# Moving LSH bit rows from SBUF straight into the operand tile, one transfer per bit, for pairs 1 to 5

## The chip, the cores and the metric

The kernel runs on one core of one Trainium2 chip. The metric is device time in microseconds (us), lower is better. Executions of one kernel spread by about one per cent here, so a ratio below 1.01 means little by itself; intervals are given at 95%. One execution of each kernel was taken by the profiler; "the profile" and "the trace" are of that one.

## The reference

Two stages. Attention over 4 batches, 8 heads, 768 tokens, 64 elements a head: a query sees only the keys that share its 6-bit hash.

```python
q_bits = (np.einsum('bhsd,dk->bhsk', q, proj) > 0)          # same for k_bits
mask = q_bucket[:, :, :, None] == k_bucket[:, :, None, :]   # all 6 bits agree
scores = np.where(mask, scale * np.matmul(q, k.transpose(0, 1, 3, 2)), -1e9)
attn = softmax(scores); out = np.matmul(attn, v)
```

Its output, as 3072 tokens of 512, goes through a feed-forward part: `h = max(max(x @ w1, x @ w2), x @ w3)`, then `h @ w_out`, with 768 hidden units.

## The kernel before

The mask costs no work on the scores: the 6 bits, coded as plus or minus a large number, stand as 6 extra rows below the 64 rows of q and k in the operand tile `T`, so that the score matmul adds a large constant for each bit that agrees, and the exponential takes away all but full agreement. Heads are worked on in pairs (16 of them, 4 to a batch; "pair 4" is the first of the second batch). Per pair: load q and k (fp32), split each into two fp16 parts (VectorE and ScalarE), transpose on TensorE into `T`, multiply by the projection (`hps`), compare with zero on VectorE (`bit`), transpose the bits (`bps`), shift and scale them (`bt`), and bring these rows into partitions 64 to 69 of `T`. The rows have to come from 72 partitions into 6 others, and two transfers do it, through DRAM:

```python
    def hash_bits(b, pr, e):
        ...
        nc.vector.tensor_tensor(out=bit[:].rearrange("p n a k -> p (n a) k"), in0=hv[:, :, 0:NBITS], in1=neg[:],
                                op=AluOp.is_gt)          # 128 x (q/k, chunk, bit): the bit runs fastest

    def bit_T(b, pr, e):                                 # TensorE: two transposes of 128 x 72
        ...
    def bit_evac(b, pr, e):                              # VectorE: bt, 72 x 2 x 128
        ...
    def bit_out(b, pr, e):
        drs[b, pr] = dram.tile([2, R, P], FP16, tag="dr", name="dr")
        nc.sync.dma_start(drs[b, pr][:].rearrange("n r t -> r n t"), bts.pop((b, pr))[:])

    def bit_in(b, pr, e):
        nc.sync.dma_start(T[b, pr][D : D + NBITS, :, :],
                          drs.pop((b, pr))[:].rearrange("n (a k) t -> k (n a) t", k=NBITS))
```

The kernel carries its own list scheduler: each piece is a task with an engine, an assumed duration, a priority and its buffers, and a simulated clock decides the order in which each engine's instructions are written down. On the chip that order is fixed, and each engine executes what is written for it in that order. The tasks concerned:

```python
        bo = add(("SP", 0.65), p0 + 7, [be], lambda e: bit_out(b, pr, e), take=("dr",), give=("bt",), xfer=0.05,
                 after=[last_copy[0]])
        bi = add(("SP", 0.65), p0 + 7, [bo], lambda e: bit_in(b, pr, e), give=("dr",), xfer=0.25, ...)
        # loads of q, k, v of later batches are issued on the same queue, behind the bits of an earlier pair:
        loads[n, b, pr, (0, 2)] = add(("SP", 0.5), ..., after=[last_load[0], bounced[g], ...])
```

The softmax here doesn't subtract the row's maximum and nothing guards it: scores larger than these inputs give would overflow.

## Time and profile before

| | before |
|---|---|
| time, median of 3 | 268.71 us (267.62 to 270.26) |
| span of the profiled run | 265.3 us |
| TensorE busy | 97% |
| pair 1's bits ready, its first scores | 18.9 us, 26.38 us |
| next batch's first loads issued (q, k; the following v) | 26.96, 27.41; 32.84 us |
| first layer-1 matmul of the feed-forward part | 48.74 us |
| one comparison (`bit`) on VectorE | 0.31 us |

In the lines below, L and a number is a line of that kernel, SPq the queue of SyncE that issues transfers (it works in order, and its times are issue times, not transfer times); `out<-in` names the tiles; a bracket is idle time of that engine just before, with what ended it. Tiles named often: `s` the fp16 parts of q and k ("splits"), `tps` transposes, `sc` scores, `AT` their exponentials, `av` attend, `svp` and `vsum` the sum of v that is added with a small weight ("mean"), `ps` and `po` layers 1 and 2 of the feed-forward part. A "unit" is one pair of score matmuls with its exponential. The prediction shows the lines of before on which it rests.

### The profile page before, as it was taken

The page shows a single profiled execution, that of the slowest core. Times are in us where ns is not written, and L with a number is a line of the kernel's source. Part 1 is how long each engine was busy: PE and PEld are TensorE (multiplying, and loading weights), DVE is VectorE, ACT ScalarE, POOL GpSimd, SP SyncE. Part 2 cuts the span into 40 slices and gives each one's busy share as a digit, 9 for nine tenths or more (in the row PEclk, how much of TensorE's full clock was granted, in tenths as well). Part 3 has the DMA queues.
Part 4 walks back from the last instruction along what each step waited for, and adds up shares of the span by engine and source line. Part 5 has one row for each costly group of instructions (what it writes and reads, how often), then busy time and mean ns, then how long its engine had stood idle before and what let it go on. Part 6 is the DMA issues. An engine that isn't in the chain of part 4 may idle for free.

```text
span 265.3 us, 7323 instructions
## 1 busy us (share of the span) xinstructions
PE 257.1 (97%) x2992; PEld 174.8 (66%) x2992; DVE 174.4 (66%) x394; ACT 196.2 (74%) x283; POOL 43.0 (16%) x57
## 2 busy tenths in 40 slices
PE   7997999999999999999999999999999999999995
PEld 7886777767656666676666767766666656565552
DVE  5999489999747897468984795551655526255260
ACT  5897799997926889989989899888898632332322
POOL 1421063273310334003321030000000000000000
PEclk9999799999999999999999999999999999999999
DMA  7994489799998798989896885302030060120303
GB/s 225 340 271 80 132 278 261 236 210 325 228 216 264 209 245 199 231 226 202 172 228 186 233 173 106 70 14 97 24 62 0 4 178 4 40 79 0 121 0 120
DMA packets 67409, 41.69 MB, mean 157 GB/s; under 512 B 48047, under 2 KB 63663, under 8 KB 67375
## 3 DMA queue, kind: packets, MB, share of 16 engines
q1 hardware_dynamic: 64654, 39.26, 57.3%
q0 software_dynamic: 2640, 1.97, 4.8%
q8 instruction: 23, 0.38, 0.6%
q14 instruction: 12, 0.09, 0.1%
q10 hardware_dynamic: 80, 0.00, 0.0%
HBM read 25.72 MB, written 6.84 MB: 123 GB/s over the span
## 4 chain that ended last, share of the span: by engine, by line
PE 80%; DMA 8%; ACT 4%; POOL 2%; SPq 2%; DVE 1%; issue 1%; ACTq 0%; POOLq 0%
PE ps L478 31%; PE sc L395 21%; PE po L496 11%; PE av L413 11%; DMA v<-in_v_dram 5%; ACT AT L401 3%; PE hps L312 3%; DMA ws<-in_moe_w_out_dram 2%; SPq L250 2%; PE tps L292 1%; DMA T<-dr 1%; POOL vt L363 1%; ACT T L202 1%; PE bps L339 1%; DVE xn L449 0%
## 5 line engine op out<-in xcount | busy, mean ns | idle before, releaser
L401 ACT ACTIVATE AT<-sc 128x768 f16<-128x768 f32 x192 | 146.3, 815 | 15.9 <-PE sc L395 14.0
L478 PE MATMUL ps<-xT,w_sb 128*128 128x384 f16 x576 | 106.3, 326 | 0.1
L395 PE MATMUL sc<-T 128*128 128x384 f16 x384 | 94.0, 328 | 2.4 <-DMA T<-dr 1.4
L487 DVE TENSOR_TENSOR ht<-ht,ps 128x384 f16<-128x384 f16 x96 | 52.9, 551 | 46.6 <-PE ps L478 44.2
L413 PEld LDWEIGHTS <-AT 128*128 128x128 f16 x1152 | 60.1, 98 | 23.1 <-issue 0.7
L478 PEld LDWEIGHTS <-w_sb 128*128 128x128 f16 x576 | 52.7, 98 | 30.3 <-issue 0.2
L413 PE MATMUL av<-vone,AT 128*128 128x65 f16 x1152 | 66.0, 194 | 0.0
L395 PEld LDWEIGHTS <-T 128*128 128x128 f16 x384 | 30.3, 98 | 12.9 <-DMA T<-dr 1.6
L496 PE MATMUL po<-wout_sb,ht 128*128 128x512 f16 (+1 forms) x150 | 33.8, 370 | 0.5 <-POOL wout_sb L204 0.5
L202 ACT CAST ht<-ps 128x384 f16<-128x384 f32 x28 | 13.4, 479 | 26.4 <-DVE ht L487 19.1
L202 ACT COPY osb<-po 128x512 f32<-128x512 f32 (+1 forms) x24 | 13.6, 567 | 18.7 <-PE po L496 18.6
L363 POOL TENSOR_TENSOR vt<-v 128x384 f32<-128x384 f32 x12 | 13.8, 1149 | 65.3 <-DMA v<-in_v_dram 59.2
L430 DVE TENSOR_TENSOR t<-av,mv 128x390 f32<-128x390 f32 x32 | 18.0, 561 | 9.0 <-PE av L413 8.8
L496 PEld LDWEIGHTS <-ht 128*128 128x128 f16 x150 | 14.1, 98 | 14.3 <-DVE rr L436 0.8
L449 DVE TENSOR_TENSOR xn<-t,rr 128x384 f16<-128x384 f32 x32 | 20.0, 625 | 1.1
L273 DVE SCALAR_TENSOR_TENSOR s<-q,s 128x384 f16<-128x384 f32 x32 | 19.0, 609 | 2.5 <-ACT s L266 2.3
L273 DVE SCALAR_TENSOR_TENSOR s<-k,s 128x384 f16<-128x384 f32 x32 | 19.1, 615 | 0.2
L204 DVE CAST ht<-ps 128x384 f16<-128x384 f32 x20 | 11.1, 554 | 10.0 <-PE ps L478 9.7
L292 PE MATMUL tps<-iden,s 128*128 128x128 f16 x168 | 13.3, 219 | 0.9 <-DVE bit L322 0.3
L292 PEld LDWEIGHTS <-s 128*128 128x128 f16 x168 | 10.4, 98 | 2.2 <-DVE s L273 1.1
L312 PEld LDWEIGHTS <-T 128*128 128x128 f16 x336 | 10.0, 96 | 1.0
L312 PE MATMUL hps<-PAB,T 128*128 128x12 f16 x336 | 10.4, 168 | 0.0
(54 smaller groups left out, 141.5 us busy)
## 6 DMA issues: line engine op xcount, KB each, us to landing
v<-in_v_dram SPq DMA_DIRECT2D x16, 384.0 KB
out_dram<-osb SPq DMA_DIRECT2D x23, 256.0 KB
q<-in_q_dram SPq DMA_DIRECT2D x15, 384.0 KB
k<-in_k_dram SPq DMA_DIRECT2D x15, 384.0 KB
w_sb<-in_moe_w_dram POOLq DMA_DIRECT2D x5, 384.0 KB, 10.4
ws<-in_moe_w_out_dram SPq DMA_DIRECT2D x3, 512.0 KB
ws<-in_moe_w_dram SPq DMA_DIRECT2D x2, 384.0 KB
dr<-bt SPq DMA_DIRECT2D x15, 36.0 KB
```

Of the source, the lines that this page charges most:

```text
L202: nc.scalar.copy(o, i)
L273: nc.vector.scalar_tensor_tensor(out=s[:, a0:a1, D : 2 * D], in0=raw_view(n, b, pr, heads), scalar=QS, in1=s[:, a0:a1, 0:D], op0=AluOp.mul ...
L292: nc.tensor.transpose(p16[:, c * P : (c + 1) * P], S16[b, pr][:, a0 + c, :], iden[:])
L312: nc.tensor.matmul(o, T[b, pr][:, a, :], PAB[:], start=True, stop=True)
L395: nc.tensor.matmul(sc[:, i, 0:HQ], t[:, NA2 + hh * NCH + 2 * j + i, :], t[:, hh * NCH + hf * CH : hh * NCH + (hf + 1) * CH, :], start=True ...
L401: nc.scalar.activation(AT[:], scs.pop(u)[:, :, 0:HQ], ActFn.Exp, bias=EXP_BIAS, scale=EXP_SCALE)
L413: nc.tensor.matmul(av[:, o : o + D + 1], AT[:, i, c * P : (c + 1) * P], vones[b % 2][:, 2 * pr + hh, 2 * j + i, 0 : D + 1], start=slot == ...
L430: nc.vector.tensor_tensor(out=t[:, :, :, 0 : D + 1], in0=av[:, :, :, 0 : D + 1], in1=mv, op=AluOp.add)
L449: nc.vector.tensor_tensor(out=xv, in0=t[:, :, :, 0:D], in1=rr[:].to_broadcast([P, 2, CH, D]), op=AluOp.mult)
L478: nc.tensor.matmul(ps[:, 0:HQ], w_sb[i][:, jc, fb * P : (fb + 1) * P], xTs[b, hf][:, jc, :], start=jc == 0, stop=jc == NJ - 1)
L487: nc.vector.tensor_tensor(out=ht[:], in0=ht[:], in1=ps[:, 0:HQ], op=AluOp.max)
L496: nc.tensor.matmul(ps[:, m0:m1], hts[b, hf, fb][:, c * P : (c + 1) * P], wout_sb[:, fb, m0:m1], start=fb == 0, stop=fb == NF - 1)
```

## The change

Its intent: pair 1's scores wait for two transfers in a row. With the bits laid out bit-major, one bit's 24 rows of 128 lie in 24 partitions of `bt` in the order in which one partition of `T` wants them, so that one transfer from SBUF to SBUF places a whole row, without DRAM between. Six transfers replace two, for pairs 1 to 5; the others keep the way through DRAM.

```diff
+    direct = (1, 2, 3, 4, 5)
+
+    def by_chunk(b, pr, bit):
+        if 4 * b + pr not in direct:
+            return bit[:]
+        return bit[:].rearrange("p n a k -> p (n a k)").rearrange("p (k n a) -> p n a k", k=NBITS, n=2)
...
-        nc.vector.tensor_tensor(out=bit[:].rearrange("p n a k -> p (n a) k"), in0=hv[:, :, 0:NBITS], in1=neg[:],
-                                op=AluOp.is_gt)
+        nc.vector.tensor_tensor(out=by_chunk(b, pr, bit), in0=hv[:, :, 0:NBITS].rearrange("p (n a) k -> p n a k", n=2),
+                                in1=neg[:].rearrange("p (n a) k -> p n a k", n=2), op=AluOp.is_gt)
...
+    def bit_move(b, pr, e):
+        bt = bts.pop((b, pr))
+        for i in range(NBITS):
+            h, r = divmod(i, NBITS // 2)
+            nc.sync.dma_start(T[b, pr][D + i : D + i + 1, :, :], bt[r * NA : (r + 1) * NA, h, :])
...
+        if 4 * b + pr in direct:
+            bi = add(("SP", 1.9), p0 + 7, [be], lambda e: bit_move(b, pr, e), give=("bt",), xfer=0.3,
+                     after=[last_copy[0]])
+        else:
             bo = add(("SP", 0.65), ...)          # as before
             bi = add(("SP", 0.65), ...)
```

The scheduler is told 1.9 us for six issues, and with that the order of all engines is planned anew.

More of the change, by code (lines that the diff above doesn't have):

```diff
@@ L319, in hash_bits0 @@
             bits[0, pr] = bit
-            nc.vector.tensor_scalar(out=bit[:], in0=hv, scalar1=0.0, scalar2=None, op0=AluOp.is_gt)
+            nc.vector.tensor_scalar(out=by_chunk(0, pr, bit), in0=hv, scalar1=0.0, scalar2=None, op0=AluOp.is_gt)
             return
@@ L338, in bit_T @@
         for n in range(2):
-            nc.tensor.transpose(p16[0:R, n * P : (n + 1) * P], bit[:, n, :, :].rearrange("p a k -> p (a k)"), iden[:])
+            nc.tensor.transpose(p16[0:R, n * P : (n + 1) * P], bit[:, n, :, :].rearrange("p x y -> p (x y)"), iden[:])
     def bit_evac(b, pr, e):
@@ L627, in prep @@
         be = add(("DVE", 0.28), p0 + 6, [bT], lambda e: bit_evac(b, pr, e), take=("bt",), give=("mm",))
-        bo = add(("SP", 0.65), p0 + 7, [be], lambda e: bit_out(b, pr, e), take=("dr",), give=("bt",), xfer=0.05,
-                 after=[last_copy[0]])
-        bi = add(("SP", 0.65), p0 + 7, [bo], lambda e: bit_in(b, pr, e), give=("dr",), xfer=0.25, pad=3 if 4 * b + pr > 5 else 0.0)
+        if 4 * b + pr in direct:
+            bi = add(("SP", 1.9), p0 + 7, [be], lambda e: bit_move(b, pr, e), give=("bt",), xfer=0.3,
+                     after=[last_copy[0]])
+        else:
+            bo = add(("SP", 0.65), p0 + 7, [be], lambda e: bit_out(b, pr, e), take=("dr",), give=("bt",), xfer=0.05,
+                     after=[last_copy[0]])
+            bi = add(("SP", 0.65), p0 + 7, [bo], lambda e: bit_in(b, pr, e), give=("dr",), xfer=0.25, pad=3 if 4 * b + pr > 5 else 0.0)
         bounced[b, pr] = last_copy[0] = bi
```

## The prediction

> **What bounds the kernel now.** I read the page first (busy shares, the forty slices, the chain that ended last), then the timelines of TensorE, ScalarE and the DMA-issuing queue from 8 to 80 us, then one-microsecond windows around the one hole they show.
>
> Busy shares, slices and the head of the chain, from the page:
> ```profile
> PE 257.1 (97%) x2992; PEld 174.8 (66%) x2992; DVE 174.4 (66%) x394; ACT 196.2 (74%) x283; POOL 43.0 (16%) x57
> PE   7997999999999999999999999999999999999995
> ACT  5897799997926889989989899888898632332322
> PEclk9999799999999999999999999999999999999999
> PE 80%; DMA 8%; ACT 4%; POOL 2%; SPq 2%; DVE 1%; issue 1%; ACTq 0%; POOLq 0%
> ```
> TensorE looks full everywhere, but its slices overlap pipelined matmuls, so 97% is not a proof. In the chain, a pair of score matmuls steps by 0.33 us, six attend matmuls by 0.18, six transposes by 0.34, four layer-1 matmuls by 0.65. From about 48.7 us (first layer-1 matmuls) to the drain the timeline is these steps nearly back to back: the feed-forward part fills every gap that attention leaves. **So after 48.7 us TensorE is the bound, and only less work for it or an earlier start of that phase can shorten the run.** Before it there is attention alone, and ScalarE's exponentials (about 0.75 us each when contiguous) set the pace. The slices that stand out are PEclk's fifth (7; 26.5 to 33 us, as a slice is 6.6 us) and ScalarE's fourth and fifth (7). ScalarE's timeline, with start and duration ahead of each group and idle time behind:
> ```profile
> 24.25 0.80 ACT L202 COPY T<-tps 128x768 f16<-128x768 f16 x1
> 26.97 1.51 ACT L401 ACTIVATE AT<-sc 128x768 f16<-128x768 f32 x2 [1.93 <-PE sc L395]
> 28.78 0.81 ACT L401 ACTIVATE AT<-sc 128x768 f16<-128x768 f32 x1 [0.30 <-PE sc L395]
> 30.08 0.81 ACT L401 ACTIVATE AT<-sc 128x768 f16<-128x768 f32 x1 [0.48 <-PE sc L395]
> 31.26 3.70 ACT L401 ACTIVATE AT<-sc 128x768 f16<-128x768 f32 x5 [0.38 <-PE sc L395]
> ```
> ScalarE loses 1.93 + 0.30 + 0.48 + 0.38 = 3.09 us to scores that came late. TensorE's timeline says why, and the queue's timeline has the two transfers behind it:
> ```profile
> 26.38 0.82 PE L395 MATMUL sc<-T 128*128 128x384 f16 x4 [1.45 <-DMA T<-dr]
> ```
> ```profile
> 18.92 0.38 SPq L349 DMA_DIRECT2D dr<-bt  x1
> 23.99 0.28 SPq L352 DMA_DIRECT2D T<-dr  x1
> 24.35 0.30 SPq L349 DMA_DIRECT2D dr<-bt  x1
> 26.65 0.26 SPq L352 DMA_DIRECT2D T<-dr  x1
> 26.96 0.40 SPq L250 DMA_DIRECT2D q<-in_q_dram  x1
> 30.88 0.32 SPq L349 DMA_DIRECT2D dr<-bt  x1
> 32.50 0.29 SPq L352 DMA_DIRECT2D T<-dr  x1
> ```
> This is pair 1's round trip through DRAM: out at 18.92, the queue held until 23.99 for it to land, back in by 26.38, when the scores go. It holds the queue too: pair 2's bits are ready at 23.66 (start 23.38 + 0.28 of its bt) and go out only at 24.35, and a later load only at 26.96. The windows add a second cost, the columns being busy time and count per engine, granted clock, DMA share and GB/s:
> ```profile
> 23.00:24.00 1.00, 0.85 (x18) 0.77 (x15) 1.00 (x3) 1.00 (x2) 0.00 (x0) 1.00 0.10 15
> 25.00:26.00 1.00, 0.00 (x0) 0.00 (x0) 0.93 (x4) 0.04 (x1) 0.00 (x0) 1.00 0.30 67
> 28.00:29.00 1.00, 1.00 (x12) 0.75 (x10) 0.63 (x3) 0.70 (x2) 0.00 (x0) 0.56 0.91 266
> 29.00:30.00 1.00, 1.00 (x13) 0.66 (x11) 0.36 (x1) 0.59 (x1) 0.00 (x0) 0.50 1.05 366
> ```
> TensorE stands still for one whole window, and soon afterwards its clock is halved for about 3.4 us.
>
> **What the Trainium skill says.** (1) DMA: Bandwidth & Descriptors, section on the anatomy of one DMA: about 2 us of fixed cost, mostly the receipt of the last write, heaviest where the target is HBM (given for the GpSimd path). The trace agrees in size: in a quiet stretch the way out takes 32.50 - 30.88 = 1.62 us and the way in 26.38 - 23.99 = 2.39. (2) Same page, section on why a DMA increments its semaphore by 16: the slowest dimension not of size one decides how many engines work, the largest number up to 16 that divides it on both sides. The transfer back has 6 rows, so 6 engines; a new one-bit transfer has 24 rows of 128 on both sides, so 12. No view of before shows the second. (3) TensorE: Matmul & The Clock Gate, part 1: half the clock after an idle window of some 3.4 us. Here idleness of 1.45 us in a thin stretch was enough for windows of 0.50.
>
> **The change, part by part.**
> - *Bit-major layout.* The same DVE instructions (15 comparisons, 15 evacuations) with another write order; the comparisons take 0.30 to 0.31 us now. Estimate: at most 0.1 us more for each of five, off the path. The matrix transposes stay two per pair.
> - *Removed, for pairs 1 to 5:* one way out, one wait of the queue for it, one way in. For pair 1 the second way is 2.39 us on the path. For the others it is 1.6 to 2.9 us of latency, mostly with slack: pair 4 leaves at 41.91 and returns with an issue at 47.25, yet it is needed only at unit 48.
> - *Added:* six issues a pair. An issue of this queue takes 0.26 to 0.38, with its gap about 0.36, so 6 x 0.36 = 2.2 us instead of 0.38 + 0.28 = 0.66 us of issue. Pair 1's six go from 18.92 to about 21.1. They queue on the same engines behind the loads, as the way out does now, so I have the last one land when the way out lands now, at about 24.0 (window 23 to 24: the engines are nearly empty). **That is 26.38 - 24.0 = 2.4 us earlier.**
> - *Moved:* the order listing shows the scheduler moved work too. The unit that waits (number 13, from one) now stands behind 12 transposes that before ended at about 24.05, and the mean and attend matmuls that filled 24.05 to 24.76 come after it. TensorE should hardly stand still. Between units 13 and 36 ScalarE loses about a copy (five copies and casts of 0.7 to 0.8 us before; four and a short one after), worth about 0.35 us. First layer-1 matmuls: behind unit 36 instead of 37.
> - *Later phase:* matmul counts are equal kind by kind (5986 rows in both), so from the first layer-1 matmul on the same work follows.
>
> Sum: ScalarE needs 48.5 - 26.97 = 21.5 us from the late unit to unit 38, 1.16 of it idle; starting at 25.05 (end of its copy) without idleness it is there 1.93 + 1.16 = 3.1 us earlier, 3.4 with the lighter mix. Check from TensorE: in 24.76 to 48.74 I count 25 score pairs (8.1 us), 25 attends (4.6), 48 transposes (2.7), and 3.3 us of the rest: 18.7 of 24.0 us. So **3.1 fits into its 5.3 us of slack, and 5.3 us (2.0%) is about the most that this change can give.** I take off 0.5 us: the loads of the next batch's first pair go out only after pair 2's six issues, at about 26.3 instead of 26.96, while their consumers move 3 us forward. They should land near 29.3, and DVE, which executes in order, would meet them about then. Net 2.7 us: 268.7 - 2.7 = 266.0 us.
>
> **Rivals.**
> - *A, the wait stays.* The six small transfers stick among loads and weights (the DMA share is 1.2 to 1.3 from 15 to 21 us, and the way out needed 5.07 us) and the last lands near 26. For: 72 rows in six pieces, the last issued 2.2 us later. Against: DMA is nearly idle from 23. Then 268.5.
> - *B, the queue becomes the bound.* 5 x (2.2 - 0.66) = 7.7 us more of issue on the in-order queue, and loads behind it slip. Against: it also stops waiting 5.1, 2.3, 1.6 and 5.3 us for landings. If the loads cost more than they gain: 268 to 270.
> - *C, a new wait at unit 60.* Pair 6 still goes through DRAM. Before, 28 layer-1 matmuls cover its arrival; the new order leaves 12 there, so 16 x 0.163 = 2.6 us less cover. If it arrives no earlier: about 268.6.
> - *D, all slack goes.* With the clock kept up and DVE on time: 263.4.
> - *E, hidden anyway.* Against it stand the 1.45 us of waiting and ScalarE's 3.09 us.
>
> **Range and chances.** 266.0 is my main case; C or B in part gives 268 to 269, D 263.5. The three runs of before spread over 2.6 us, so I hold 263.6 to 268.8 for eight in ten. Over 2% faster means under 263.3, more than the counted slack: 0.06. Over 2% slower needs B and C together, 274: 0.03. Within 2%: 0.91.
>
> **What would show it.** In the timeline of the changed kernel: six issues from 18.9 to about 21; scores of unit 13 at 24 to 24.5 with no idleness over 0.5 us; ScalarE without its 1.93 us hole; no window of half clock near 28 to 31; first layer-1 matmuls at 45.5 to 46.5 instead of 48.7; then a span shorter by as much. The prediction is wrong if unit 13 still waits past 25.5 (A), if the next batch's loads or DVE's splits hold TensorE at 29 to 33 (B), or if the gain is there at 46 us and lost near unit 60 (C).

## The result, and the profile after

| | before | after |
|---|---|---|
| time, median of 4 runs on the same chip | 268.16 us (267.11 to 270.26) | 276.58 us (274.62 to 278.27) |
| span of the profiled run | 265.3 us | 274.6 us |
| first layer-1 matmul | 48.74 us | 53.62 us |

The ratio is **1.030 (1.021 to 1.040): slower by 3%**, where 1% faster was predicted. Here and below a ratio is the mean time of one kernel's fast runs over that of the other's of the same rounds, so not quite the ratio of the medians quoted.

The page of after, same rows as shown of before:
```profile
PE 260.8 (95%) x2992; PEld 176.7 (64%) x2992; DVE 176.1 (64%) x389; ACT 199.8 (73%) x288; POOL 41.8 (15%) x57
PEclk9999797999999999999999999999999999999999
PE 77%; DMA 10%; SPq 5%; POOL 2%; ACT 2%; DVE 1%; issue 1%; POOLq 0%; ACTq 0%
```
Busy times are almost the same; what is new is waiting. In the chain that ended last, the issuing queue went from 2% to 5% and transfers from 8% to 10%, TensorE down from 80% to 77%. The clock still has its 7, and a second one after it. The queue's timeline of after, with start, duration and count of each group of issues:
```profile
20.44 10.33 SPq L358 DMA_DIRECT2D T<-bt  x12
30.82 0.51 SPq L250 DMA_DIRECT2D q<-in_q_dram  x1
33.07 4.66 SPq L358 DMA_DIRECT2D T<-bt  x6
37.83 0.45 SPq L250 DMA_DIRECT2D v<-in_v_dram  x1
47.71 4.68 SPq L358 DMA_DIRECT2D T<-bt  x6
```
Six issues take 4.66 us. (The 12 at the front are pairs 1 and 2 in a row.) So the next batch's q is asked for at 30.82 instead of 26.96, 3.9 us later, and the v behind pair 3 at 37.83 instead of 32.84, 5.0 us later. Meanwhile the DMA engines have nothing to do: from 25 to 30 us their share in the windows view is 0.04. The moves' own line, with durations in ns as least, median and most:
```profile
L358 SPq DMA_DIRECT2D T<-bt x30: 732/732/1519, 20.4 to 60.7; - x30
```
What the late loads do, in the timelines of VectorE, ScalarE and TensorE of after:
```profile
42.23 0.58 DVE L268 TENSOR_SCALAR s<-q 128x768 f16<-128x768 f32 x1 [2.13 <-DMA q<-in_q_dram]
44.05 0.84 ACT L266 ACTIVATE s<-k 128x768 f16<-128x768 f32 x1 [2.30 <-DMA k<-in_k_dram]
...
27.50 0.80 PE L408 MATMUL sc<-T 128*128 128x384 f16 x2 [1.64 <-DMA T<-bt]
43.59 0.51 PE L292 MATMUL tps<-iden,s 128*128 128x128 f16 x6 [1.30 <-DVE s L273]
70.27 0.22 PE L389 MATMUL svp<-vsum,ones 128*128 128x130 f16 x1 [1.18 <-POOL vsum L379]
```
The splits wait for q and k (this q went out at 38.33, behind pair 3's six; in before its like went out at 33.27), TensorE's transposes wait for the splits, and at 70 us a mean of v comes late. The wait that was to vanish is still there: pair 1's scores stand 1.64 us for the bits (1.45 before). From its bits to its scores it takes 7.1 us (20.4 to 27.5) where the two transfers took 7.5 (18.9 to 26.4).

Last, the comparisons, first of before and then of after (line 320 became 327, line 332 became 339):
```profile
L332 DVE TENSOR_TENSOR bit<-hps,neg x14: 307/307/309, 22.2 to 169.6; 128x144 f16<-128x144 f32 x14
L320 DVE TENSOR_SCALAR bit<-hps x1: 296/296/296, 17.3 to 17.3; 128x144 f16<-128x144 f32 x1
```
```profile
L339 DVE TENSOR_TENSOR bit<-hps,neg x14: 307/308/799, 23.5 to 177.5; 128x144 f16<-128x144 f32 x14
L327 DVE TENSOR_SCALAR bit<-hps x1: 811/811/811, 18.5 to 18.5; 128x144 f16<-128x144 f32 x1
```
The same 144 elements take 0.80 us instead of 0.31 when each write lands 48 bytes from the last.

**A sum over TensorE's records** helps in what follows. In a quiet stretch, a matmul's start follows the one before by a nearly fixed step: about 0.0313 us behind an attend, 0.1625 behind a score or a layer-1 matmul, 0.2155 behind a layer-2 one, 0.056 behind a transpose, 0.0243 behind a hash matmul. The sum of these steps is the work of a phase; what the phase takes beyond it is lost to waiting or to the halved clock. Profiled runs, in us:

| | first score | lost from there to the first layer-1 matmul | lost from there to the last matmul | span |
|---|---|---|---|---|
| before | 11.06 | 6.2 | -0.2 | 265.3 |
| after | 12.47 | 10.4 | 3.4 | 274.6 |

The three differences, 1.4 + 4.2 + 3.6 = 9.2, make up the 9.3 us between the spans (the kernels differ by 0.7 us in how much work stands before the first layer-1 matmul, and that cancels). The first, the start, is no effect of the change: the instructions until then are the same, and first scores came at 11.06 to 13.11 us in fast profiled runs, with a load that landed sooner or later. It is one reason not to read a difference of a microsecond from two profiles.

### The profile page after: what moved, and what is told of

Same layout as the page of the kernel before. It is cut to its first block, busy times and chain, and to the rows that moved or that the text cites.

```text
span 274.6 us, 7370 instructions
## 1 busy us (share of the span) xinstructions
PE 260.8 (95%) x2992; PEld 176.7 (64%) x2992; DVE 176.1 (64%) x389; ACT 199.8 (73%) x288; POOL 41.8 (15%) x57
## 4 chain that ended last, share of the span: by engine, by line
PE 77%; DMA 10%; SPq 5%; POOL 2%; ACT 2%; DVE 1%; issue 1%; POOLq 0%; ACTq 0%
PE ps L491 32%; PE sc L408 19%; PE po L509 11%; PE av L426 10%; DMA q<-in_q_dram 5%; SPq L358 4%; PE hps L312 2%; DMA ws<-in_moe_w_dram 2%; DMA ws<-in_moe_w_out_dram 2%; ACT AT L414 1%; DMA T<-bt 1%; POOL vt L376 1%; PE tps L292 1%; SPq L250 1%; PE hps L310 1%
## 5 line engine op out<-in xcount | busy, mean ns | idle before, releaser
L491 PEld LDWEIGHTS <-w_sb 128*128 128x128 f16 x576 | 52.0, 98 | 31.0 <-issue 2.1
L408 PEld LDWEIGHTS <-T 128*128 128x128 f16 x384 | 30.8, 98 | 15.7 <-issue 4.8
L273 DVE SCALAR_TENSOR_TENSOR s<-q,s 128x384 f16<-128x384 f32 x32 | 21.6, 699 | 3.8 <-ACT s L266 3.7
L462 DVE TENSOR_TENSOR xn<-t,rr 128x384 f16<-128x384 f32 x32 | 19.2, 600 | 1.1
L292 PE MATMUL tps<-iden,s 128*128 128x128 f16 x168 | 14.4, 229 | 2.8 <-DVE s L273 1.8
L204 DVE CAST ht<-ps 128x384 f16<-128x384 f32 x19 | 10.5, 554 | 9.9 <-PE ps L491 9.8
L292 PEld LDWEIGHTS <-s 128*128 128x128 f16 x168 | 11.2, 103 | 4.3 <-DVE s L273 3.4
L202 ACT CAST vone<-v 128x768 f16<-128x768 f32 x12 | 10.1, 839 | 1.2 <-DMA v<-in_v_dram 1.2
```

Of the source, the lines that this page charges most:

```text
L202: nc.scalar.copy(o, i)
L273: nc.vector.scalar_tensor_tensor(out=s[:, a0:a1, D : 2 * D], in0=raw_view(n, b, pr, heads), scalar=QS, in1=s[:, a0:a1, 0:D], op0=AluOp.mul ...
L292: nc.tensor.transpose(p16[:, c * P : (c + 1) * P], S16[b, pr][:, a0 + c, :], iden[:])
L408: nc.tensor.matmul(sc[:, i, 0:HQ], t[:, NA2 + hh * NCH + 2 * j + i, :], t[:, hh * NCH + hf * CH : hh * NCH + (hf + 1) * CH, :], start=True ...
L462: nc.vector.tensor_tensor(out=xv, in0=t[:, :, :, 0:D], in1=rr[:].to_broadcast([P, 2, CH, D]), op=AluOp.mult)
L491: nc.tensor.matmul(ps[:, 0:HQ], w_sb[i][:, jc, fb * P : (fb + 1) * P], xTs[b, hf][:, jc, :], start=jc == 0, stop=jc == NJ - 1)
```

## The experiments

The theory going in: the queue's issue time delays the loads behind it, and that is the loss. Rivals: the slower comparisons on VectorE are; or the newly planned order is, whatever the transfers cost. They ran in four batches, each on one chip with runs of before between (medians 268.02, 266.99, 267.85 and 267.70 us of 7, 7, 11 and 7 runs). The expectations name theories; where a result met none of them, the text says so.

### What an issue costs (probe_issue)

Before, with small transfers in groups of four appended after the last store. Its span means nothing (282.4 us).

```diff
+    for i in range(4):   # 24 partitions -> 1 partition, as the change does it
+        nc.sync.dma_start(spare[i : i + 1, :, :], ones[0:NA, :])
+    for i in range(4):   # SBUF -> DRAM
+        nc.sync.dma_start(d1[i, :, :], ones[0:NA, :])
+    for i in range(4):   # DRAM -> SBUF
+        nc.sync.dma_start(spare[4 + i : 5 + i, :, :], d1[i : i + 1, :, :])
+    ...                  # 24 -> 24 partitions, 8 rows, 16 rows, 1 -> 1 partition; from ScalarE, from GpSimd
```

> The kernel before, with small transfers added behind its last store, four of each kind, so that the queue's time for each issue can be read alone, while the transfer engines are nearly idle. Queue theory: the 0.73 us that a one-bit transfer takes to issue belongs to its pattern (24 rows of 24 partitions into one partition), so it is 0.73 here too; the kinds that the kernel before has (rows to DRAM, DRAM to rows) take 0.28 to 0.35; a transfer of 8 rows takes less than one of 24 if the cost goes with rows. Contention theory: the issue is held by loads in flight, so here it takes about 0.3 for every kind. The span is some 20 us longer; that means nothing.

The lines of four of the groups, durations in ns as least, median and most:
```profile
L779 SPq DMA_DIRECT2D xn<-ones x4: 732/733/897, 262.7 to 265.6; - x4
L781 SPq DMA_DIRECT2D d<-ones x4: 352/364/528, 266.3 to 267.7; - x4
L783 SPq DMA_DIRECT2D xn<-d x4: 214/214/215, 268.2 to 269.1; - x4
L785 SPq DMA_DIRECT2D xn<-ones x4: 713/720/785, 269.4 to 271.8; - x4
```
The same 6 KB cost 0.73 us of issue with SBUF on both sides, 0.36 from SBUF to DRAM, 0.21 from DRAM to one row of SBUF. It isn't the single target partition (24 to 24 partitions: 0.72), hardly the number of rows (8 rows 0.64, 16 rows 0.58, one partition to one partition 0.59), nor a crowd (the 24 to 24 group ran alone, from 269 us on). From ScalarE's queue it is 0.77, at the same time as the first group; from GpSimd's 0.54, but that queue was free early and issued them at 155 us, in the middle of the kernel. Why both sides in SBUF cost more was not found.

### VectorE's writes alone (dve_major)

After, with the loops turned: VectorE reads with a stride and writes contiguously. Same layout, same order of instructions.

```diff
-            ... tensor_tensor(out=by_chunk(b, pr, bit), in0=hv[...].rearrange("p (n a) k -> p n a k", n=2), ...
+            ... tensor_tensor(out=bit[:]...rearrange("p (k m) -> p k m", k=NBITS),
+                              in0=hv[:, :, 0:NBITS].rearrange("p a k -> p k a"), in1=neg[:].rearrange("p a k -> p k a"), ...
```

> The changed kernel, but the comparisons read their operands bit-major and write contiguously; the order of all instructions and the 30 one-bit transfers stay. Theory DVE (the write with a stride of 48 bytes made five comparisons take 0.80 instead of 0.31 us, on a nearly full engine, and that costs the time): the comparisons go back to 0.3 to 0.4 us and the time to about 269 to 271. Queue theory: 275 to 276, a gain of at most 1.5 us, as five times 0.49 us of DVE sits beside 4.7 us of issue a pair.

```profile
L341 DVE TENSOR_TENSOR bit<-hps,neg x4: 407/410/418, 22.9 to 51.4; 128x144 f16<-128x144 f32 x4
```
0.41 us instead of 0.80, and 0.295 for the one-input form, as before. The ratio is 1.020 (1.013 to 1.026). About one per cent of the three belongs to the writes, and two stay: between the two expectations, so neither theory has all of it. (The strided reads are of `hps`, in PSUM, and of `neg`, in SBUF.)

### The new order with the old transfers (order_bounce)

```diff
     def bit_move(b, pr, e):
-        bt = bts.pop((b, pr))
-        for i in range(NBITS): ...
+        bit_out(b, pr, e)
+        bit_in(b, pr, e)
```

> The order of the changed kernel on every engine, with the two transfers through DRAM and the bit layout of the kernel before. Order theory (the scheduler, given other costs, made an order that is bad in itself): 275 or more. Queue theory: near the kernel before, 267 to 271, since the queue is again held only for landings.

1.026 (1.021 to 1.031), 275.2 us: what the order theory expected, and not the queue theory. So the order that after uses loses nearly as much with the old transfers, old layout and old comparisons. The losses are other ones. TensorE's timeline of this kernel:
```profile
26.57 0.82 PE L406 MATMUL sc<-T 128*128 128x384 f16 x2 [2.19 <-DMA T<-dr]
...
66.38 0.22 PE L387 MATMUL svp<-vsum,ones 128*128 128x130 f16 x1 [1.35 <-POOL vsum L377]
79.32 0.82 PE L489 MATMUL ps<-xT,w_sb 128*128 128x384 f16 x4 [1.35 <-DMA xT<-xn]
```
The order has less work ahead of pair 1's scores, as if they came early (a mean and two groups of attend matmuls stand behind them now). Here they come as late as in before (26.57 against 26.38), so TensorE stands 2.19 us instead of 1.45. In the sum over records it loses 7.5 us before the first layer-1 matmul and 5.8 after it. These later waits (1.35, 1.35, and 0.79 at 57 us) are small and of different kinds, and I could not lead all 5.8 us back to one of them.

### The old order with the new transfers (old_order_moves)

Before, with the comparisons of the change and the six moves put where the way out stood, nothing at the way back; no row differs in the order of the four compute engines.

```diff
     def bit_out(b, pr, e):
+        if 4 * b + pr in direct:
+            for i in range(NBITS): ... nc.sync.dma_start(T[b, pr][D + i : D + i + 1, :, :], bt[r * NA : (r + 1) * NA, h, :])
+            return
```

> The kernel before with its own order on the four compute engines (no row differs), where pairs 1 to 5 send their bits by the six one-bit transfers at the place of the way out, with the bit-major comparisons of the change. With the run of the new order and old transfers it completes a square of two orders and two ways. Queue theory: about 275 to 278, like the change. Order theory: about 268 to 271, as the transfers are innocent and pair 1's bits land some 7 us after they are ready in either way. Both partly: 271 to 275.

1.0195 (1.0145 to 1.0245). The load of q goes out at 31.33 us, and the timeline of VectorE shows who waits for it:
```profile
34.53 0.56 DVE L268 TENSOR_SCALAR s<-q 128x768 f16<-128x768 f32 x1 [3.14 <-DMA q<-in_q_dram]
```
In an order that is known to run in 267 us, the new transfers with the new comparisons cost 2% (old_order_dve below finds the comparisons to matter little here). VectorE waits twice for a late q, 3.14 and 2.48 us; the scores wait 0.70 us for pair 1's bits. The four corners are then:

| | old transfers | six moves |
|---|---|---|
| old order | 1 | 1.0195 |
| new order | 1.026 | 1.030 |

The two parts don't add, and why is open: plan47, below, was planned with the true cost and loses as much.

### Is any other order worse? (nudge_sp, plan47)

If before's order were a lucky one, any other would lose. nudge_sp is before with one planning cost altered, which moves 964 rows of TensorE's order:

```diff
-        bo = add(("SP", 0.65), p0 + 7, [be], ...
+        bo = add(("SP", 0.75), p0 + 7, [be], ...
```

> The kernel before with nothing changed but one number of its scheduler, the queue cost of the way out, 0.75 us instead of 0.65. No instruction is added or removed; 964 rows of TensorE's order differ. Order theory in the form that the order before was picked among many by trying, so any other costs time: 271 to 277. If before's order is nothing special: 267 to 270.

1.004 (0.997 to 1.010): another order, the same time. The rival in that form falls; that the order of after costs something by itself is not excluded by it. plan47 is after, with the scheduler told the true 4.7 us:

```diff
-            bi = add(("SP", 1.9), p0 + 7, [be], lambda e: bit_move(b, pr, e), ...
+            bi = add(("SP", 4.7), p0 + 7, [be], lambda e: bit_move(b, pr, e), ...
```

> The changed kernel, its scheduler told 4.7 us of queue time for six one-bit transfers (measured: 4.66) instead of 1.9. Queue theory: the queue time stays, so 273 to 277. Order theory in the form that the order is bad because it was planned with a wrong cost: 268 to 271. Order theory in the form that any order but the tuned one costs time: 272 to 278.

1.029 (1.022 to 1.037). Knowing the cost didn't help.

### More queue time in the kernel before (occupy_dram)

The test that leaves the bits alone. Before, with its layout, its order and its transfers, and six small issues nobody needs behind the way back of pairs 2 to 5. They go from SBUF to DRAM and cost 2.4 us each time.

```diff
+        if 2 <= 4 * b + pr <= 5:
+            idle = dram.tile([NBITS, NA, P], FP16, tag="idle", name="idle")
+            for i in range(NBITS):
+                nc.sync.dma_start(idle[i, :, :], ones[0:NA, :])
```

> The kernel before, its order and its way through DRAM, plus six idle issues (24 rows of ones to a DRAM tile that nothing reads, 0.36 us each to issue, 6 KB each) behind the way back of pairs 2 to 5: some 2.2 to 2.5 us more of queue time a pair, before the loads that follow. The bits are no later, DVE has nothing more to do. Queue theory: DVE and TensorE wait for q and k of the next pairs as in the run of the moves in the old order (2 to 3 us at 33 to 44 us), time 271 to 274. Theory that the moves' own lateness or the strided comparison costs the time: 267 to 269.

1.038 (1.032 to 1.045). Queue, VectorE and TensorE:
```profile
27.18 2.37 SPq L357 DMA_DIRECT2D idle<-ones  x6
29.59 0.40 SPq L250 DMA_DIRECT2D q<-in_q_dram  x1
```
```profile
34.76 0.56 DVE L268 TENSOR_SCALAR s<-q 128x768 f16<-128x768 f32 x1 [4.76 <-DMA q<-in_q_dram]
...
35.97 1.06 PE L292 MATMUL tps<-iden,s 128*128 128x128 f16 x12 [2.94 <-DVE s L273]
62.38 0.22 PE L380 MATMUL svp<-vsum,ones 128*128 128x130 f16 x1 [2.64 <-POOL vsum L370]
```
Issuing q 2.6 us later (29.59 against 26.96) brings waits of the kind seen in after, and larger, and a slowdown as large; 278 us is more than the theory expected (271 to 274). Six small transfers issued at this place suffice to lose that much. But queue time isn't all that changed. The kernel sends 36 KB more each time, and its q landed 5.2 us after its issue (29.59 to 34.76), where it took 3.3 in after (30.82 to 34.08) and 3.2 in old_order_moves: about 2 of the 4.76 us are the load's own. The packed trace has one 16 KB packet of the queue `q8 instruction` among the packets of q, which took 2.4 us from 30.69 on; in after and old_order_moves such a packet comes behind q's. That it held the load up is a guess, not tested. So the figure is no price of an issue.

### The moves on other queues (pool_moves, split_queues)

pool_moves: after, with `nc.gpsimd` in place of `nc.sync` in `bit_move`.

> The changed kernel with the 30 one-bit transfers issued by GpSimd instead of the load queue; the order on every engine stays. Queue theory: loads (1,0) go out near 24 to 27 us instead of 30.8, first layer-1 matmuls at 46 to 50 us instead of 53.6, time 266 to 271. Theory that the small transfers themselves are slow, or that the new order is bad: no change, 275 to 278. Risk: GpSimd's own casts and loads come late behind the issues, which would show as waits for vone, vsum or w_sb.

1.029 (1.022 to 1.037), not what the queue theory expected. The load queue is free, but the bits come late; TensorE:
```profile
30.83 0.82 PE L408 MATMUL sc<-T 128*128 128x384 f16 x2 [5.86 <-DMA T<-bt]
```
It's a confounded test: loads now go out early and fill the engines, and GpSimd's queue holds weight loads too; its moves land after 1.6 to 9.8 us, 3.7 in the middle. split_queues takes the old order, leaves pair 1 on the load queue and puts only pairs 2 to 5 on GpSimd's:

```diff
+                q = nc.sync if 4 * b + pr == 1 else nc.gpsimd
+                q.dma_start(T[b, pr][D + i : D + i + 1, :, :], bt[r * NA : (r + 1) * NA, h, :])
```

> The moves in the old order, those of pair 1 on the load queue as in the change, those of pairs 2 to 5 issued by GpSimd; strided comparisons as in the change. Queue theory: the loads go out at 26 to 27 instead of 31.3 us, the waits for q of 3.1 and 2.5 us vanish, time 267 to 270 (the moves in the old order: 272.8). Theory DVE or theory of slow moves: 271 to 274. Risk: GpSimd's moves queue behind its weight loads, which shows as a wait of scores for T in pairs 2 or 3.

1.020 (1.015 to 1.026), no better than the 1.0195 with all on one queue, and not what I expected. The load of q went out at 26.80, and VectorE's waits for it are gone, as the theory says; but now scores wait for bits:
```profile
34.84 0.65 PE L411 MATMUL sc<-T 128*128 128x384 f16 x2 [2.22 <-DMA T<-bt]
```
One wait was traded for another, so neither run supports the theory by its time; the first half of the mechanism, load issue to VectorE's wait, it does show.

### The comparisons in the old order (old_order_dve)

old_order_moves with the contiguous writes of dve_major.

> The moves in the old order, all on the load queue, with the comparisons that read with a stride and write contiguously (0.41 instead of 0.80 us). It tells DVE's part under the old order: theory DVE 268 to 269.5; queue theory 271 to 273, at most 1.5 us less than with the strided write (272.8), about the half us by which pair 1's and pair 2's bits are earlier each.

1.018 (1.012 to 1.024): next to nothing against 1.0195. VectorE has slack in the old order: it stands 4.84 us for q. (That is more than the 3.14 of old_order_moves, though q went out 2 us earlier, at 29.36: it landed 4.9 us after its issue, again with a packet of `q8 instruction` among its own.) That the writes cost only where VectorE is already late is how I read it.

### Keeping DRAM, with better rows (bounce_rows, bounce_rows15)

The bit-major layout, used another way: out and back through DRAM as before, but the way back reads 6 rows of 6 KB instead of 144 pieces of 256 bytes; VectorE writes contiguously. In bounce_rows for all pairs from 1 on, in bounce_rows15 only for 1 to 5.

```diff
-                          drs.pop((b, pr))[:].rearrange("n (a k) t -> k (n a) t", k=NBITS))
+                          drs.pop((b, pr))[:].rearrange("h (r m) t -> (h r) m t", m=NA))
```

> The kernel before in its own order, through DRAM, with the bit-major layout (comparisons that read with a stride and write contiguously) for pairs 1 to 15, so that the way back reads 6 rows of 6 KB instead of 144 pieces of 256 bytes. If the layout's way back lands sooner (2.39 us before, perhaps 2.0): pair 1's scores start 0.3 us earlier, time 267 to 268.5. DVE theory: 14 comparisons at 0.41 instead of 0.31 us cost 1.4 us of DVE, mostly hidden: 268 to 270.

> The kernel before in its order, through DRAM, with the bit-major layout only for pairs 1 to 5 and 6 rows of 6 KB on the way back. The run for all pairs took most of the wait at 24 to 28 us away (0.5 instead of 2.9 us of TensorE loss) and gave it back near 56 to 61 and 103 us. If those losses came from the layout of the later pairs, this one is 1 to 2 us faster than before: 265 to 267. If they are misfits of an order planned for other times, the same 268.

1.003 (0.997 to 1.009) and, over five rounds, 1.002 (0.997 to 1.007). In bounce_rows the loss between 20 and 30 us fell from 2.9 to 0.5 us, and 2.5 us were lost later instead, near 56 to 61 and 103 us. So removing the wait for pair 1's bits does not by itself shorten the run; no kernel was faster than before.

### The dose (half_new, one_new, half_old, half_new_dve)

Only some of the six moves, so the results are wrong (0.46 relative error); the same instructions run otherwise, and that no time depends on the data is assumed. Three moves cost 2.33 us, which is what the prediction had assumed for six (2.2).

```diff
-        for i in range(NBITS):
+        for i in range(3):          # one_new: range(1)
```

> The changed kernel, its own order, with only three of the six one-bit transfers a pair (wrong result on purpose: three bit rows are missing[...]). Their issue takes 3 x 0.78 = 2.3 us, the 2.2 us that the prediction had for all six. Queue theory: q and k of the next pair go out some 4.7 us earlier, the waits of DVE and ScalarE for them go, time 267 to 270. If the order of the change is bad even when the transfers cost what its scheduler was told (1.9 us): 272 to 276.

> As before it, with one one-bit transfer a pair (wrong result on purpose), 0.78 us of queue. Third point of a row of doses 1, 3, 6. Queue theory: 265 to 268, less than with three. Order theory: 272 to 276 whatever the dose.

> Three one-bit transfers a pair (wrong result on purpose) in the order of the kernel before. Queue theory: 266 to 269 against 272.8 with six. If the loss of the moves in the old order came from the layout or from late bits of pair 1: 270 to 273.

> Three one-bit transfers a pair in the changed order (wrong result on purpose), and the comparisons that write contiguously (0.41 instead of 0.80 us): both sizes near what the prediction assumed. If its mechanism was right and these two sizes were wrong: 265 to 268 (predicted 266.0). If a step beside them failed: 270 or more.

| moves per pair | new order | new order, contiguous writes | old order |
|---|---|---|---|
| 6 | 1.030 (1.021 to 1.040) | 1.020 (1.013 to 1.026) | 1.0195 (1.0145 to 1.0245) |
| 3 | 1.012 (1.005 to 1.018) | 1.0005 (0.993 to 1.008) | 1.001 (0.994 to 1.008) |
| 1 | 1.006 (0.999 to 1.013) | | |

With half of the moves q goes out at 27.60 and VectorE waits 0.88 us for it. Queue and VectorE of half_new, and its clock row:
```profile
27.60 0.51 SPq L250 DMA_DIRECT2D q<-in_q_dram  x1
30.87 0.56 DVE L268 TENSOR_SCALAR s<-q 128x768 f16<-128x768 f32 x1 [0.88 <-DMA q<-in_q_dram]
PEclk9999999999999999999999999999999999999999
```
Scores no longer wait for bits, and the half-clock stretch is gone. All columns fall with the dose, in both orders (three moves and one differ by less than their intervals). The medians of half_new (270.5) and one_new (269.0) came out 0.5 and 1 us above what the queue theory expected. Fewer issues make both the loads behind them and the bits themselves earlier, and the dose doesn't tell these two apart. Of the losses in the sum over records (first score, lost before the first layer-1 matmul, lost after it): half_new 11.60, 5.4, 1.0; one_new 12.67, 5.5, 2.6.

## Why the prediction was wrong

**What held.** TensorE is the bound after 48.7 us, and its work was the same to the instruction. Latency did not fail: pair 1's scores came 1.5 us after the end of its last issue (26.03 to 27.50), and the prediction had allowed 2.9 (21.1 to 24.0). The half clock at 28 us went with the hole (none in half_new and bounce_rows). But a hole doesn't always bring it: none followed 2.37 us of standing at the same place in dve_major, or 1.43 us in occupy_dram. Twelve engines for a one-bit transfer fit the packed trace, which has 12 packets of 4 bytes beside the 24 of 256 for each. The loads were seen to be in danger ("the loads of the next batch's first pair go out only after pair 2's six issues"), and the place where they would hurt, VectorE's splits.

**The step that failed first**: "*Added:* six issues a pair. An issue of this queue takes 0.26 to 0.38, with its gap about 0.36, so 6 x 0.36 = 2.2 us". The durations came from the transfers of the bits, with DRAM on one side (a load in the same lines takes 0.40, also from DRAM); the new ones have SBUF on both. They take 0.73 us, with the gap 0.78: 4.7 us a pair, and 24.35 us for five as measured. Everything after it slipped: the six for pair 1 ended at 26.03 instead of 21.1 (1.5 us of this because its bits were ready at 20.44 and not at 18.92, the rest because six took 5.6 us), so scores came at 27.5 and not at 24.0 to 24.5; q went out at 30.82 and not 26.3. The Trainium skill, DMA: Bandwidth & Descriptors, section "Rules for kernel authors", advises to coalesce many small transfers into one large one. The change does the opposite (two transfers of 36 KB became six of 6 KB), and this agrees with the rule: it costs 4.7 us of queue instead of 0.66. About half of the 4.7 is the number of transfers (occupy_dram's six to DRAM took 2.4), the rest their kind.

**So rival B came true**, with more than twice its size: not 7.7 but 21 us more of issue (24.35 less 5 x 0.66). The argument against it, that the queue also stops waiting 5.1 us for pair 1's landing, only broke even: six issues take as long as that wait. occupy_dram shows that six small issues a pair here are enough to lose 3 to 4%, and the dose row that most of what the change loses goes with its issues: halving them took 1.030 to 1.012, and 1.0195 to 1.001 in the old order.

**Second, "at most 0.1 us more for each of five, off the path"** was 0.49 us more, and not off the path once VectorE was late: 1.030 against 1.020 with six moves, 1.012 against 1.0005 with three, about one per cent both times (the intervals overlap a little in each pair). In the old order it was worth 0.2%, which is nothing. The Trainium skill would have warned: SBUF — State Buffer, section on the DMA port swizzle, says SBUF has lines of 16 bytes and that an access to a new line pays a penalty. I had looked for the operation and not for its stride. The trace agrees for writes 48 bytes apart (0.80 against 0.31 us); the strided reads, in part of PSUM, cost far less (0.41, and 0.295 in the one-input form, which reads PSUM alone).

**Third, the gain itself.** With both terms at the size that I had assumed, half_new_dve, the result is 1.0005 and not 0.990. The step was "ScalarE ... is there 3.1 us earlier" with "from the first layer-1 matmul on the same work follows". half_new does remove the wait, yet its loss before that matmul falls only from 6.2 to 5.4 us: ScalarE's idleness comes back in pieces of 0.2 to 0.5 us. And after it, the same work takes 1.0 us longer than its steps, where before lost nothing. The work was the same, the waiting was not: I had put that term at zero. What refilled each microsecond was not separated, as starts alone vary by more than that.

Put together in the new order: 1.8% for issues (6 to 3 moves), 1.1% for the writes, 1.0% for the gain that didn't come: 3.9%, against 276.6 - 266.0 = 10.6 us, 3.9% of 268. The sum comes out by construction, as each step starts where the last ended: it is an account in one order of taking things away, each part uncertain by about 0.8, and order_bounce shows that the parts interact.

**The other rivals.** A, the wait stays: true in part (1.64 us), from issue time and not from crowded engines. C, a wait at unit 60: no such wait of scores; the late waits are for v's means. D, all slack goes, did not appear. E, hidden anyway, had been set aside for the two waits seen; half_new_dve and the two bounce_rows kernels show that it was nearer the truth: with the pair 1 wait gone or shortened, the time stays the same.

**Left open**: why an issue with SBUF on both sides takes twice as long; how the loss by issue time divides between late loads and late bits (split_queues took the first away and got the second); and what exactly costs order_bounce 2.6%. half_new_dve, at 1.0005 in the same order, says only that this order is not slow with every set of transfers.

## What to carry to other kernels

Before one transfer is replaced by several, measure the issue time of exactly that kind, both ends included, and multiply it by what waits behind it on that in-order queue: idle DMA engines are no sign that it is free. Where a layout change is needed, let VectorE read with the stride and write contiguously. And in a statically scheduled kernel, test a change in the old order as well as in the new one: the wait that you remove may only make room for others, and a new order brings its own.

## What the Trainium skill lacked or had wrong

- DMA: Bandwidth & Descriptors, section "Issuing engines are not separate DMA queues", calls the time on the sequencer to initiate a transfer "usually small relative to the DMA itself". Here it was 0.73 us a transfer of 6 KB and 4.7 us for six, while the last of pair 1's six landed and was used within 1.5 us of the end of its issue.
- The same page's anatomy of one DMA has about 50 ns of dispatch and descriptor generation "small, variable", for GpSimd's path; runs here have 0.54 us on GpSimd's queue. It has no figure by what the two ends are: on the load queue 0.73 us SBUF to SBUF, 0.36 SBUF to DRAM, 0.21 DRAM to SBUF, for the same 24 rows of 256 bytes.
- SBUF — State Buffer has the 16-byte line but no size for the penalty, and doesn't compare writes with reads: 144 two-byte writes 48 bytes apart took 0.80 us instead of 0.31, strided reads (one input in PSUM, one in SBUF) with contiguous writes 0.41. VectorE: DVE Perf Modes doesn't point to it.
- TensorE: Matmul & The Clock Gate, part 1, gives half the clock after an idle window of about 3.4 us. In after, 1.64 us of idleness in a thin stretch was followed by windows of 0.50 from 28 to 30 us, and 1.45 us in before likewise; in half_new, without that hole, there was none. Nor was there after 2.37 us in dve_major or 1.43 us in occupy_dram, so the length of one hole alone doesn't tell.
